# Written-out order of a fused Nyström attention and SiLU layer: transposes of batch 2 by DMA, scores in halves, loads and DMA transposes of a batch listed together

## The chip, the cores and the metric

The kernel runs on one core of a Trainium2 chip, as one launch. The metric is the time of the launch on the device in microseconds; the median of three runs is 250.57 us (249.38 to 251.9). A launch that was profiled beside them took 247.08 us; in it 245.4 us lie between the first and the last instruction of the program (the span), and 1.68 us outside. Times from the profile are counted from the start of the span.

## The reference

There are 8 batches (b = 0 to 7), 8 heads, 576 tokens, 64 numbers per head. q and k are averaged over groups of 18 tokens to 32 landmarks; three softmaxes A, Bm, C follow, six Newton steps towards an inverse of Bm, and a two-layer SiLU network on the result.

```python
q_lm = q.reshape(B, H, m, S // m, D).mean(axis=3)      # m = 32
k_lm = k.reshape(B, H, m, S // m, D).mean(axis=3)
A  = sm(q, k_lm)          # 576 x 32 per head
Bm = sm(q_lm, k_lm)       # 32 x 32
C  = sm(q_lm, k)          # 32 x 576
Z  = Bm.T / (...)
for _ in range(6):
    Z = 2 * Z - Z @ Bm @ Z
attn = A @ Z @ C @ v
# x: (4608, 512), all heads of a token side by side
h = x @ w_in              # 512 -> 2048
g = h * (1.0 / (1.0 + np.exp(-h)))
out = g @ w_out           # 2048 -> 512
```

## The kernel before

Heads go in two groups of four (g = 0, 1), so that 4 heads x 32 landmarks fill 128 partitions. Per batch the stages are:

- **Loads** (line 354, `load`): q and k (`ld0.b`, `ld1.b`, 576 KB each as bf16, line 400) and v in three parts (`ldv0.b` to `ldv2.b`, 192 KB each, line 407). They are issued by GpSimd (POOL), as are the first layer's weights (`wi...`, lines 414 and 418) and the second layer's (`wo0` to `wo3`, 512 KB each, line 424). Two buffers each for q/k, transposed q/k and v serve even and odd batches.
- **Transposes** of q and k into `qT`. For batches below `NTR` = 3 TensorE does them (`tr`, line 515: 18 for q and 18 for k, in four steps each) and ScalarE or VectorE copies them out of PSUM (`trc`). From batch 3 on, four DMA transposes per batch do them, issued by SyncE (SP): `xt10`, `xt11` for k and `xt00`, `xt01` for q (line 539). C's exponentials are transposed likewise: by TensorE in batches 0 and 1, by two DMA transposes `ct0`, `ct1` (line 814) after that.
- **Landmarks**: from batch 2 on a tree of four VectorE additions over the transposed k, then q (`lra` to `lrd`, line 575), then on TensorE `ltr1.b` and `ltr0.b` (one matmul `ps<-rs,fold` each).
- **Scores**: `sb` (Bm), `A` and `C` (16 matmuls `ps<-qT,lmT` each, four PSUM banks), exponentials `Ax`, `Cx`, column sums `S`, logarithms `Ln`, and the Newton steps `ns`, `nsd`, `fb`.
- **First layer with attention folded in**: `cv` (C times v), `zt`, `m` (into w_in), then 16 pieces `h` and two `hx` per batch, with SiLU by ScalarE (`g`, `gx`).
- **Second layer**: `o0` to `o3` for the first 256 rows of batch 0; all other rows as pairs of seven products `p1` to `p7` instead of eight, whose operand sums `ss` and `wt` VectorE makes.

What sets the order is `SEQUENCE` (line 19), written out by hand or by an earlier search: a list of the names above. `Plan.run` walks it, gives out PSUM banks, and emits each piece on its engine. So each engine's instructions stand in the list's order, and every engine works strictly in its own order; between engines only semaphores count, not places in the list. `*n` in the list is n matmuls on zeros, which keep TensorE busy at the start.

A few orderings between DMAs are added as waits (`after`). A DMA transpose of batch b waits until `ldv1.b` has landed; the loads of batch b+1 (line 1096, `later_loads`) wait for the third entry of batch b's list of DMA transposes, which is `xt00.b`, and from batch 4 on also for `ct0` of two batches earlier. No such wait ties the loads `wo0` to `wo3` to anything. In `load` there is also a dependence on the load eight before (lines 362 and 363); it is only asked about when the list is walked.

Of the kernel before, what the change touches and what calls it, by code (L numbers as in the profile page):

```python
# [10 lines left out]
AF = mybir.ActivationFunctionType  # L11
# [8 lines left out]
ldk ld11.0 const ident k0cACT k0cDVE k0 *15 lms100.0 tr15.0 tr10.0 trc10.0/DVE lms106.0 lms1012.0  # L20
*6 lms110.0 lms116.0 tr114.0 lms1112.0 lmc1.0/DVE ld00.0 *6 lms000.0 tr05.0 tr00.0 trc05.0/ACT
trc114.0/ACT ltr1.0 lmT1.0/ACT trc00.0/DVE tr19.0 trc19.0/DVE trc15.0/DVE lms006.0 ld01.0
lms0012.0 lms010.0 lms016.0 lms0112.0 ld0.1 ld1.1 ldv2.0 ldv0.0 wi0b1 ldv1.0 wi0b0 tr09.0 tr014.0
lmc0.0/DVE *1 ltr0.0 lmT0.0/ACT *6 sb.0 pb.0 trc014.0/DVE trc09.0/DVE A.0 Ax01.0 Ax00.0 Ax10.0
Ax11.0 *5 C.0 Cx01.0 Cx10.0 Cx11.0 Cx00.0 pbs.0 pbr.0 bmx.0 bmt.0 csb.0 n1.0 nrm.0 tr09.1 lms000.1
lms006.1 S10.0 lms0012.1 lms010.1 bbd.0 trc09.1/DVE stz.0 f0.0 stf0.0 stf1.0 fb00.0 lms016.1
Ln10.0 S00.0 Ln00.0 fb01.0 lms0112.1 lmc0.1/DVE S01.0 ns00.0 nsd00.0 Ln01.0 S11.0 ns01.0 Ln11.0
nsd01.0 fb11.0 ctm00.0 ctc00.0/DVE tr05.1 trc05.1/ACT tr00.1 trc00.1/ACT Rs1.0 Rs0.0 ns11.0
nsd11.0 fb10.0 fb21.0 tr19.1 trc19.1/DVE ltr0.1 lms100.1 lms106.1 ns10.0 nsd10.0 lms1012.1 tr014.1
lms110.1 lms116.1 trc014.1/DVE ns21.0 tr114.1 lmT0.1/ACT wi1a wi0a wi1b1 wi1b0 wi3b0 wi3a  # L30
lms1112.1 lmc1.1/ACT tr10.1 trc10.1/ACT tr15.1 *2 ltr1.1 lmT1.1/ACT fb20.0 nsd21.0 etn1.0
trc15.1/DVE ns20.0 fb31.0 *3 ns31.0 ctm10.0 trc114.1/ACT etn0.0 nsd31.0 sb.1 pb.1 *1 A.1 Ax01.1
Ax00.1 nsd20.0 fb30.0 pbs.1 wrc.0 *1 ns30.0 nsd30.0 ctc10.0/DVE fb40.0 pbr.1 fb41.0 bmx.1 bmt.1
wi3b1 Ax11.1 Ax10.1 *5 C.1 Cx00.1 Cx11.1 Cx01.1 *1 ns40.0 nsd40.0 ns41.0 nsd41.0 fb50.0 fb51.0
cv0.0 cv1.0 wc.0 S01.1 Ln01.1 ns50.0 nsd50.0 *2 ns51.0 bbd.1 nsd51.0 zbd.0 S11.1 Ln11.1 S00.1
Ln00.1 wi2b0 wi2b1 wi2a ldv0.1 ldv1.1 *5 zt.0 ztc.0/DVE S10.1 ctm00.1 ctc00.1/DVE Rs0.1 Ln10.1
Cx10.1 *2 m1.0 mc11.0/ACT mc10.0/DVE m0.0 f0.1 mc01.0/DVE mc00.0/ACT *1 ctm10.1 ctc10.1/DVE Rs1.1
csb.1 *1 h4.0 n1.1 m3.0 nrm.1 stz.1 stf0.1 mc31.0/DVE fb00.1 g4.0 mc30.0/DVE h2.0 g2.0 h6.0 g6.0
h0.0 g0.0 h3.0 ns00.1 wrc.1 nsd00.1 fb10.1 h5.0 g5.0 m2.0 mc21.0/ACT mc20.0/DVE *1 h13.0 g13.0
ns10.1 nsd10.1 fb20.1 h15.0 hx0.0 g15.0 ns20.1 nsd20.1 fb30.1 h9.0 g9.0 h11.0 g11.0 etn0.1 ns30.1  # L40
nsd30.1 fb40.1 hx8.0 gx8.0 g3.0 h8.0 h12.0 g12.0 etn1.1 ns40.1 nsd40.1 fb50.1 gx0.0 h10.0 g10.0
ld1.2 tr15.2 trc15.2/DVE h14.0 g14.0 ns50.1 nsd50.1 zbd.1 ldv2.1 cv0.1 wc.1 tr114.2 trc114.2/DVE
tr19.2 trc19.2/DVE zt.1 g8.0 ztc.1/ACT tr10.2 trc10.2/DVE lra1.2 h7.0 g7.0 m3.1 mc31.1/ACT
mc30.1/ACT m1.1 mc11.1/DVE mc10.1/ACT h1.0 g1.0 ld0.2 tr00.2 lrb1.2 tr09.2 tr014.2 trc014.2/DVE
tr05.2 trc05.2/DVE trc09.2/DVE lrc1.2 trc00.2/ACT h12.1 g12.1 h7.1 g7.1 h15.1 m2.1 mc20.1/ACT m0.1
mc00.1/ACT mc21.1/ACT mc01.1/ACT wo0 o0@5001.0 h14.1 g14.1 g15.1 o0@5000.0 fold lrd1.2 lra0.2
lrb0.2 lrc0.2 lrd0.2 h11.1 g11.1 ltr0.2 ltr1.2 lmT1.2/DVE lmT0.2/ACT ss00@5020.0 ss10@5020.0
ss20@5020.0 ss30@5020.0 wo1 h5.1 o1@5000.0 sb.2 pb.2 pbs.2 pbr.2 bmx.2 bmt.2 wo2 wt00 bbd.2 h8.1
h3.1 o1@5001.0 o2@5000.0 wo3 o2@5001.0 wt01 g8.1 csb.2 o3@5001.0 oc@5001.0/ACT g3.1 g5.1 n1.2
nrm.2 stz.2 o3@5000.0 hx8.1 f0.2 gx8.1 h0.1 g0.1 oc@5000.0/ACT h2.1 h10.1 g10.1 h4.1 h1.1 g2.1  # L50
g1.1 wt11 wt21 stf0.2 fb00.2 ns00.2 h13.1 g13.1 wt31 nsd00.2 fb10.2 wt10 wt20 wt30 p1@5020.0
c1@5020.0/ACT ns10.2 nsd10.2 fb20.2 h9.1 h6.1 g4.1 g9.1 g6.1 ss00@5100.0 p5@5020.0 c5@5020.0/DVE
hx0.1 gx0.1 ss10@5100.0 l1done.0 C.2 Cx00.2 Cx10.2 p6@5020.0 u2@5020.0/DVE ld1.3 ldv1.3 xt10.3
xt11.3 ns20.2 nsd20.2 ss20@5100.0 p3@5020.0 c12@5020.0 p7@5020.0 ld0.3 xt01.3 xt00.3 ldv0.2 ldv2.2
ldv1.2 l1done.1 A.2 Ax01.2 Cx11.2 ct1.2 Ax10.2 Ax11.2 p1@5100.0 c1@5100.0/ACT Ax00.2 Cx01.2 ct0.2
os@5000.0 ld1.4 lra1.3 fb30.2 ns30.2 p2@5020.0 ss30@5100.0 lrb1.3 os@5001.0 S10.2 S11.2 Ln11.2
Ln10.2 Rs1.2 p6@5100.0 S01.2 Ln01.2 S00.2 Ln00.2 p5@5100.0 nsd30.2 lrc1.3 fb40.2 lrd1.3 ltr1.3
c22@5020.0 lra0.3 u2@5100.0/DVE lrb0.3 p4@5020.0 ns40.2 lrc0.3 lrd0.3 ltr0.3 c11@5020.0 etn1.2
nsd40.2 c5@5100.0/ACT p3@5100.0 Rs0.2 lmT1.3/ACT etn0.2 lmT0.3/ACT sb.3 c12@5100.0 c21@5020.0/ACT
p7@5100.0 pb.3 pbs.3 pbr.3 fb50.2 A.3 Ax11.3 cv0.2 ldv1.4 c22@5100.0 wrc.2 wc.2 ld0.4 ldv0.3  # L60
ldv2.3 ldv2.4 ns50.2 nsd50.2 Ax10.3 Ax00.3 S11.3 Ln11.3 Ax01.3 p2@5100.0 C.3 Cx00.3 Cx01.3 Cx10.3
zbd.2 zt.2 ztc.2/ACT S10.3 Ln10.3 p4@5100.0 Cx11.3 ss00@5120.0 c11@5100.0 os@5100.0 ss10@5120.0
ss20@5120.0 p1@5120.0 S01.3 Ln01.3 m3.2 mc31.2/ACT bmx.3 wrc.3 mc30.2/DVE c21@5100.0/ACT os@5101.0
ct1.3 m2.2 mc21.2/DVE mc20.2/ACT bmt.3 p5@5120.0 S00.3 m0.2 m1.2 mc11.2/DVE csb.3 bbd.3 n1.3 nrm.3
stz.3 c1@5120.0/ACT p6@5120.0 u2@5120.0/DVE mc01.2/ACT mc10.2/ACT Rs1.3 Ln00.3 Rs0.3 mc00.2/ACT
h14.2 f0.3 h12.2 p2@5120.0 stf0.3 fb00.3 ns00.3 nsd00.3 c5@5120.0/DVE fb10.3 c11@5120.0 g12.2
p7@5120.0 h7.2 g7.2 ns10.3 nsd10.3 h4.2 h5.2 h8.2 g8.2 g5.2 fb20.3 ns20.3 h10.2 g10.2 c22@5120.0
p4@5120.0 c21@5120.0/ACT nsd20.3 fb30.3 ns30.3 hx0.2 nsd30.3 fb40.3 h15.2 gx0.2 g15.2 ns40.3
nsd40.3 ct0.3 xt00.4 ld1.5 ldv0.4 h9.2 g9.2 g14.2 h1.2 h0.2 g1.2 g0.2 cv0.3 ldv1.5 fb50.3
ss30@5120.0 ns50.3 wc.3 nsd50.3 zbd.3 ld0.5 h11.2 g11.2 h13.2 g4.2 g13.2 h3.2 g3.2 etn1.3 zt.3  # L70
ztc.3/DVE etn0.3 p3@5120.0 c12@5120.0 m3.3 mc30.3/ACT m0.3 mc01.3/DVE mc00.3/ACT m2.3 mc21.3/ACT
m1.3 mc20.3/ACT h2.2 hx8.2 g2.2 h6.2 g6.2 mc31.3/DVE h12.3 gx8.2 h3.3 h10.3 mc10.3/DVE mc11.3/DVE
h7.3 h2.3 g2.3 h4.3 g4.3 g10.3 h13.3 h5.3 g5.3 hx8.3 gx8.3 g13.3 h9.3 h11.3 g7.3 h14.3 h6.3 g6.3
g11.3 p1@5200.0 g3.3 h8.3 g8.3 ss00@5200.0 p5@5200.0 hx0.3 g14.3 g9.3 ss00@5220.0 xt11.4 xt01.4
xt10.4 ss10@5200.0 lra1.4 lrb1.4 lrc1.4 ss10@5220.0 ss20@5220.0 lrd1.4 lra0.4 lrb0.4 os@5020.0
ss20@5200.0 l1done.2 ltr1.4 h1.3 h0.3 g0.3 g1.3 g12.3 h15.3 gx0.3 c1@5200.0/DVE p6@5200.0
u2@5200.0/ACT os@5021.0 ss30@5200.0 c5@5200.0/DVE p3@5200.0 ss30@5220.0 lmT1.4/DVE lrc0.4 lrd0.4
ltr0.4 lmT0.4/ACT g15.3 p1@5220.0 sb.4 pb.4 c1@5220.0/ACT xt11.5 xt10.5 c12@5200.0 lra1.5 lrb1.5
lrc1.5 p7@5200.0 c22@5200.0 lrd1.5 p2@5200.0 c11@5200.0 p4@5200.0 c21@5200.0/ACT C.4 Cx11.4 Cx10.4
Cx01.4 p6@5220.0 u2@5220.0/ACT Cx00.4 p5@5220.0 c5@5220.0/ACT A.4 Ax01.4 Ax10.4 Ax00.4 Ax11.4  # L80
pbs.4 pbr.4 bmx.4 xt01.5 xt00.5 lra0.5 csb.4 ss00@5300.0 p1@5300.0 S10.4 ltr1.5 p7@5220.0 lrb0.5
ss10@5300.0 ss20@5300.0 lrc0.5 n1.4 nrm.4 wrc.4 lrd0.5 ltr0.5 lmT0.5/ACT S00.4 p3@5220.0 l1done.3
os@5120.0 os@5121.0 Ln10.4 os@5200.0 ct0.4 ld0.6 stz.4 c1@5300.0/ACT bmt.4 lmT1.5/DVE bbd.4 f0.4
sb.5 pb.5 stf0.4 S11.4 Ln11.4 Rs1.4 p2@5220.0 S01.4 Ln01.4 fb00.4 ns00.4 c22@5220.0 pbs.5
c11@5220.0 c12@5220.0 Ln00.4 p5@5300.0 c5@5300.0/ACT Rs0.4 p4@5220.0 c21@5220.0/ACT pbr.5
p6@5300.0 u2@5300.0/ACT etn1.4 ss30@5300.0 bmx.5 bmt.5 bbd.5 csb.5 etn0.4 nsd00.4 n1.5 fb10.4
ss00@5320.0 p3@5300.0 ss00@5340.0 ct1.4 cv0.4 ldv1.6 C.5 Cx00.5 Cx10.5 Cx11.5 Cx01.5 ns10.4
nsd10.4 p7@5300.0 p1@5320.0 nrm.5 fb20.4 ns20.4 wc.4 c12@5300.0 c22@5300.0 stz.5 nsd20.4 p2@5300.0
A.5 Ax10.5 Ax00.5 c1@5320.0/ACT p5@5320.0 ss10@5320.0 fb30.4 ns30.4 ss20@5320.0 f0.5 stf0.5
p4@5300.0 Ax01.5 Ax11.5 S11.5 Ln11.5 c21@5300.0/ACT p6@5320.0 u2@5320.0/ACT nsd30.4 fb40.4 ns40.4  # L90
S01.5 Ln01.5 ss30@5320.0 fb00.5 S10.5 p2@5320.0 Ln10.5 Rs1.5 nsd40.4 fb50.4 ns50.4 c11@5300.0
p7@5320.0 nsd50.4 zbd.4 zt.4 ss10@5340.0 ns00.5 nsd00.5 c11@5320.0 fb10.5 p1@5340.0 ztc.4/ACT
# [1070 lines left out]
```

## Time and profile before

| | us |
|---|---|
| median of three runs (lowest, highest) | 250.57 (249.38, 251.9) |
| the profiled launch | 247.08 |
| its span | 245.4 |
| ScalarE busy | 180.8 |
| VectorE busy | 180.0 |
| TensorE weight loads, beside matmuls | 165.8 |
| GpSimd busy | 36.7 |

Busy times are unions over an engine's instructions, so an engine that is busy 180 of 245 us may still be the bound in one stretch. A matmul's shown duration includes its way through the pipeline: what it costs in a dense row is the distance from its start to the next one's. The same holds for ScalarE and VectorE, whose neighbours overlap by about 0.1 us. Loads by GpSimd and stores and transposes by SyncE use the same 16 DMA engines through two queues, q0 and q1:

```profile
q0 software_dynamic: 15120, 18.06, 45.1%
q1 hardware_dynamic: 39808, 17.35, 34.9%
```

The columns are packets, megabytes, and the share of 16 engines' span.

### The profile page before, as it was taken

To read this page: it belongs to the slowest core of one execution; us is meant where nothing else is said; L and a number is where in the kernel's file an instruction comes from. 1 tells how busy PE (TensorE), PEld (TensorE's weight loads), DVE (VectorE), ACT (ScalarE), POOL (GpSimd) and SP (SyncE) were. 2 spreads that over 40 slices of the span, in tenths; PEclk is the share of its full clock that TensorE was granted. 3 is DMA by queue.
4 is the path that set the end of the run, shared out by engine and by line. 5 is a ranking of instruction groups with operands and counts; after the bars stand their busy time and mean duration, and the time that the engine had idled before them with its cause. 6 is when DMAs were issued, how large, how long until landed. Compare 5 with 4: busy or idle time off the path is not lost.

```text
span 245.4 us, 7471 instructions
## 1 busy us (share of the span) xinstructions
PE 233.3 (95%) x2948; PEld 165.8 (68%) x2948; DVE 180.0 (73%) x503; ACT 180.8 (74%) x432; POOL 36.7 (15%) x62
## 2 busy tenths in 40 slices
PE   7999999999999999199999999999999999999992
PEld 5986464457867556067878754777876765789882
DVE  2589889789998591489798968938899475348752
ACT  3299999988989998159746699999779788634100
POOL 8346713000050040000130060000000000000000
PEclk9999999999999999769999999999999999999999
DMA  6999999999999999793999999985414421012343
GB/s 160 207 203 197 206 207 206 210 205 204 132 177 220 202 137 178 185 194 98 136 190 171 167 185 239 190 145 136 108 47 117 121 52 39 1 43 77 88 119 109
DMA packets 55876, 36.84 MB, mean 150 GB/s; under 512 B 36640, under 2 KB 47392, under 8 KB 55840
## 3 DMA queue, kind: packets, MB, share of 16 engines
q0 software_dynamic: 15120, 18.06, 45.1%
q1 hardware_dynamic: 39808, 17.35, 34.9%
q10 hardware_dynamic: 912, 0.95, 1.4%
q8 instruction: 23, 0.38, 0.6%
q14 instruction: 13, 0.11, 0.1%
HBM read 36.70 MB, written 9.44 MB: 188 GB/s over the span
## 4 chain that ended last, share of the span: by engine, by line
PE 78%; ACT 7%; DMA 7%; SPq 3%; issue 1%; DVE 1%; ACTq 0%; DVEq 0%
PE ps L325 74%; DMA qT<-qk 6%; PE ps L515 3%; SPq L539 2%; ACT gm L913 2%; DMA gm<-in_k_dram 1%; ACT L913 1%; SPq L814 1%; ACT L1116 1%; ACT gx L936 1%; ACT m L335 1%; PE ps L802 1%; DVE red L575 1%; ACT pb L641 1%; ACT et L742 0%
## 5 line engine op out<-in xcount | busy, mean ns | idle before, releaser
L913 ACT ACTIVATE gm<-ps 128x512 f16<-128x512 f32 x128 | 68.7, 621 | 15.0 <-PE ps L325 14.3
L325 PE MATMUL ps<-etn,m 128*128 128x512 bf16 (+1 forms) x512 | 73.5, 289 | 0.2
L325 PEld LDWEIGHTS <-gm 128*128 128x128 f16 x512 | 48.6, 98 | 12.5 <-issue 1.3
L325 PE MATMUL ps<-w_out_sb,gm 128*128 128x256 f16 (+1 forms) x392 | 53.0, 281 | 0.0
L325 PEld LDWEIGHTS <-ss 128*128 128x128 f16 x408 | 39.5, 99 | 9.8 <-issue 1.8
L325 PEld LDWEIGHTS <-m 128*128 128x128 bf16 x512 | 31.5, 98 | 20.8 <-issue 3.2
L325 PE MATMUL ps<-wt,ss 128*128 128x256 f16 x272 | 35.5, 276 | 0.2
L1036 DVE TENSOR_TENSOR ost<-ost,ps 128x256 f32<-128x256 f32 x51 | 20.9, 416 | 13.4 <-PE ps L325 7.4
L335 ACT COPY ost<-ps 128x256 f32<-128x256 f32 (+1 forms) x45 | 17.2, 388 | 10.9 <-PE ps L325 10.6
L335 ACT CAST m<-ps 128x512 bf16<-128x512 f32 x36 | 19.4, 612 | 1.1 <-PE ps L325 0.8
L337 DVE CAST m<-ps 128x512 bf16<-128x512 f32 x28 | 18.3, 685 | 2.3 <-PE ps L325 1.9
L710 DVE SCALAR_TENSOR_TENSOR st<-st,ps 128x128 bf16<-128x128 bf16 (+2 forms) x54 | 13.6, 257 | 8.5 <-PE ps L325 5.5
L407 POOL DMA_DIRECT2D v<-in_v_dram x24 | 14.0, 590 | 30.8 <-DMA qT<-qk 13.6
L325 PE MATMUL ps<-w_out_sb,ss 128*128 128x256 f16 x136 | 17.5, 273 | 0.0
L325 PE MATMUL ps<-wt,gm 128*128 128x256 f16 x120 | 15.5, 272 | 0.0
L575 DVE TENSOR_TENSOR red<-qT 128x1024 f16<-128x1024 bf16 x12 | 8.3, 689 | 9.4 <-DMA qT<-qk 9.2
L685 DVE TENSOR_TENSOR fb<-st,hmask 128x256 bf16<-128x256 bf16 (+1 forms) x54 | 14.4, 271 | 0.8
L752 ACT ACTIVATE ln<-ps 128x288 f32<-128x288 f32 x32 | 12.4, 423 | 2.7 <-PE ps L325 2.4
L787 ACT ACTIVATE ce<-ps 128x288 bf16<-128x288 f32 x32 | 13.0, 424 | 1.7 <-PE ps L325 1.6
L1001 DVE TENSOR_TENSOR ss<-gm 128x1024 f16<-128x1024 f16 x15 | 10.2, 686 | 5.2 <-ACT gm L913 5.2
L742 ACT ACTIVATE et<-ps 128x288 bf16<-128x288 f32 x32 | 11.1, 423 | 3.6 <-PE ps L325 3.6
L337 DVE COPY ost<-ps 128x256 f32<-128x256 f32 x25 | 10.5, 420 | 3.2 <-PE ps L325 3.0
(93 smaller groups left out, 332.0 us busy)
## 6 DMA issues: line engine op xcount, KB each, us to landing
out_dram<-ost SPq DMA_DIRECT2D x126, 64.0 KB, 2.1
v<-in_v_dram POOLq DMA_DIRECT2D x24, 192.0 KB, 10.0
qk<-in_q_dram POOLq DMA_DIRECT2D x7, 576.0 KB, 10.6
qk<-in_k_dram POOLq DMA_DIRECT2D x7, 576.0 KB, 9.2
w_out_sb<-in_moe_w_out_dram POOLq DMA_DIRECT2D x4, 512.0 KB, 15.1
w_in_sb<-in_moe_w_in_dram POOLq DMA_DIRECT2D x8, 128.0 KB, 7.2
w_in_sb<-in_moe_w_in_dram POOLq DMA_DIRECT2D x4, 256.0 KB, 9.0
out_dram<-ost ACTq DMA_DIRECT2D x10, 64.0 KB, 1.7
```

The source lines that it names most:

```text
L325: nc.tensor.matmul(out=out_ap, lhsT=lhsT, rhs=rhs, start=start, stop=stop, skip_group_check=True)
L335: nc.scalar.copy(out=out, in_=in_)
L337: nc.vector.tensor_copy(out=out, in_=in_)
L407: lambda e, a=a: nc.gpsimd.dma_start(out=v_r[b % 2][a * L:(a + 1) * L, :, :], in_=v[b].rearrange("h (l a x) d -> a l h (x d)", l=L, a=VA)[ ...
L575: lambda e: nc.vector.tensor_tensor(out=o_, in0=a_, in1=b_, op=OP.add),
L685: nc.vector.tensor_tensor(out=fb[it % 2][:, g0:g1], in0=bc(sr[it % 3][:, g0:g1, 0:L], 4, 2), in1=bc(hmask, n, 1), op=OP.mult), [o], 14.5 + ...
L710: nc.vector.scalar_tensor_tensor(out=s2[:, g0:g1, lo:SW], in0=s[:, g0:g1, lo:SW], scalar=2.0, in1=ps[:, 0:NG * SW].rearrange("p (g x) -> p ...
L742: lambda e, g=g, et=et, c=c: nc.scalar.activation(out=et[:, c], in_=bank(me["A"], 2 * g + c)[:, 0:HS], func=AF.Exp, scale=sc / J),
L752: lambda e, g=g, c=c, ln=ln: nc.scalar.activation(out=ln[:, c], in_=bank(me["S", g, c])[:, 0:HS], func=AF.Ln),
L787: nc.scalar.activation(out=ce[:, :, 0:VP].rearrange("p (i c) (a l) -> p c a i l", c=2, a=VA)[:, c], in_=bank(me["C"], 2 * g + c)[:, 0:HS]. ...
L913: lambda e, dc=dc, cell=cell: nc.scalar.activation(out=gm[:, dc, :], in_=bank(cell["o"]), func=AF.Silu),
L1036: nc.vector.tensor_tensor(out=out_, in0=x, in1=y, op=OP.add)
```

## The change

`NTR` goes from 3 to 2, so batch 2 gets DMA transposes `xt10.2` to `xt01.2` in place of 36 TensorE transposes and 8 copies out of PSUM. `A` and `C` become two pieces per batch, one per head group, with two PSUM banks and 8 matmuls each. The dependence on the load eight before goes. Three estimates of duration, which only the list's maker uses, change. And the whole list is another one, with 56 matmuls on zeros instead of 64.

```diff
-    NTR = 3
+    NTR = 2
...
-        if len(swdge) >= 8:
-            d.append((swdge[-8], None))
...
-        use = [prev2[x] for x in ("A", "C") if x in prev2]
+        use = [prev2[x, g] for x in "AC" for g in range(NG) if (x, g) in prev2]
...
-        def am(e):
-            for g in range(NG):
+        for g in range(NG):
+            def am(e, g=g):
                 for h in range(4):
                     for c in range(2):
-                        mm(bank(me["A"], 2 * g + c)[L * h:L * h + L, 0:HS],
+                        mm(bank(me["A", g], c)[L * h:L * h + L, 0:HS],
...
-                    lmT_all + ([] if cr else [(pb_op, -0.2)]) + qt_ops[0, 0] + qt_ops[0, 1] + ready, p0 + 20,
-                    psum=4, tiled="q")
+                           lmT_all + ([] if cr else [(pb_op, -0.2)]) + qt_ops[0, g] + ready, p0 + 20,
+                           psum=2, tiled="q")
```

C changes in the same way. Of the list, the stretches around the two places that the prediction speaks of are these. Before, batch 2 and the second layer's weights:

```
... ld1.2 tr15.2 trc15.2/DVE h14.0 ... lra1.2 h7.0 ... ld0.2 tr00.2 lrb1.2 ...
... wo0 o0@5001.0 h14.1 g14.1 g15.1 o0@5000.0 fold lrd1.2 lra0.2
lrb0.2 lrc0.2 lrd0.2 h11.1 g11.1 ltr0.2 ltr1.2 lmT1.2/DVE ... wo1 ... wo2 ... wo3 ...
```

After:

```
... h7.1 g12.1 ld1.2 ld0.2 ldv0.2 ldv1.2 xt10.2 xt11.2 lra1.2 lrb1.2 lrc1.2 lrd1.2 xt00.2 xt01.2
lra0.2 lrb0.2 lrc0.2 lrd0.2 wo0 o0@5001.0 g9.1 h10.1 g10.1 h0.1 g11.1 g0.1 g2.1 g7.1 ss00@5100.0
ss10@5100.0 ss20@5100.0 ss30@5100.0 ltr1.2 lmT1.2/ACT wo2 wo1 wt00 o0@5000.0 o1@5000.0 o2@5000.0
ltr0.2 lmT0.2/ACT o1@5001.0 sb.2 pb.2 wo3 wt01 ...
```

SP's order of the transposes of batch 4 was `xt00.4 xt11.4 xt01.4 xt10.4`, with `ld1.5` listed right after the first; it becomes `xt10.4 xt11.4 xt00.4 xt01.4`, with `ld1.5 ld0.5 ldv0.5 ldv1.5 ldv2.5 ct0.4 ct1.4 cv0.4` in a row much later. GpSimd's order of loads becomes: k and q of batch 0, k and q of batch 1, `wi3` and v of batch 0, `wi2`, `wi0`, `wi1` and v of batch 1, then `ld1.2 ld0.2 ldv0.2 ldv1.2 wo0 wo2 wo1 wo3 ldv2.2 ld1.3 ...`.

## The prediction

> **What bounds the kernel now.** First the page's busy times and its 40 slices (6.1 us each; a digit is a tenth of the slice):
>
> ```profile
> PE 233.3 (95%) x2948; PEld 165.8 (68%) x2948; DVE 180.0 (73%) x503; ACT 180.8 (74%) x432; POOL 36.7 (15%) x62
> ...
> PE   7999999999999999199999999999999999999992
> ...
> PEclk9999999999999999769999999999999999999999
> ```
>
> TensorE (PE) is the bound throughout, with one hole in slice 17 and a lower granted clock in the two slices after. The waits of PE say what made the hole (total, times, longest):
>
> ```profile
> PE ps L325 <- DVE rs L575: 5.4, 1, 5.4
> ```
>
> The chain of waits (start, length, what) leads back from it:
>
> ```profile
> 86.72 14.41 DMA qT<-qk
> ...
> 101.23 0.70 DVE red L575
> ...
> 104.17 15.06 PE ps L325 x139
> ```
>
> A transpose of batch 4's k, `xt10.4`, was issued at 86.72 and took 14.41 us to land; the tree on VectorE (DVE) waited for it, `ltr1.4` for the tree. The table by stretches (length, then busy time and count of PE, PEld, DVE, ACT, POOL, granted clock, DMA share, GB/s) shows the price:
>
> ```profile
> 40.00:65.00 25.00, 25.00 (x235) 15.22 (x233) 21.73 (x58) 23.13 (x53) 1.16 (x2) 1.00 1.19 193
> 65.00:98.00 33.00, 32.79 (x444) 21.17 (x443) 23.24 (x64) 30.34 (x72) 6.31 (x10) 1.00 1.11 180
> 98.00:104.00 6.00, 0.75 (x19) 0.61 (x17) 2.70 (x6) 1.19 (x3) 0.00 (x0) 0.79 0.77 184
> 104.00:108.50 4.50, 4.33 (x16) 2.19 (x16) 4.40 (x11) 2.06 (x4) 0.00 (x0) 0.52 1.08 202
> ```
>
> Between starts of matmuls I count 5.6 us lost in the hole, and 2.0 us in the four pieces after it at half clock (three `h` at 0.85 instead of 0.43, one `p` at 1.58 instead of 0.87). The old stall is worth 7.6 us.
>
> Why did that transpose take so long? `ld1.5` waits for `xt00.4` alone, and that stood first on SP; so the loads of batch 5 (issued from 86.34) ran beside `xt10.4`, which stood last. Against it, how transposes go otherwise (issues by SP: start, length, count):
>
> ```profile
> 52.28 8.58 SPq L539 DMA_TRANSPOSE qT<-qk  x4
> ...
> 101.64 6.21 SPq L539 DMA_TRANSPOSE qT<-qk  x4
> ```
>
> The four from 101.64, with no load in flight, landed at 105.4, 106.9, 108.5 and 109.9. The four from 52.28 landed at 59.2, 60.2, 63.1, 64.1: three loads of v were still in flight until 58.2, and the first transpose came 1.0 us after them. `xt10.4` came 0.2 us after the last load beside it (100.9). In both rows a transposing DMA beside loads lands when the loads are through.
>
> **The change, part by part.**
>
> *The old stall.* In the new list `xt00` is third on SP, and `ct0` of two batches earlier is also waited for; only `xt01` can meet the next loads, and q's tree comes later than k's. I take the whole 7.6 us off.
>
> *36 transposes on PE.* 9 in 0.50 us, so 2.0 us; 8 matmuls on zeros fewer at 0.11 make 0.9. All of it lies before `ltr1.2`. The 8 copies (seven on DVE at 0.42 to 0.48, one on ACT at 0.59) also go, from a stretch where both are nearly full (21.73 and 23.13 of 25 us).
>
> *What takes their place* is the point of this prediction. `ltr1.2` now needs four DMAs and a tree, and the list cannot hold the weights' loads behind them: `wo0`, `wo2`, `wo1`, `wo3` have no wait on a transpose, and POOL issues them as early as the queue lets it. Here is how that went before, in POOL's timeline (start, length, count) and in the page's DMA issues (KB each, us to landing):
>
> ```profile
> 27.91 2.28 POOL L424 DMA_DIRECT2D w_out_sb<-in_moe_w_out_dram  x3
> 30.35 0.75 POOL L424 DMA_DIRECT2D w_out_sb<-in_moe_w_out_dram  x1 [0.16 <-issue]
> ```
>
> ```profile
> w_out_sb<-in_moe_w_out_dram POOLq DMA_DIRECT2D x4, 512.0 KB, 15.1
> ```
>
> They stand issued 12 to 18 us ahead of landing, in a queue that is full. So I add the queue up. Before, `ld0.2` landed at 37.8, then the four `wo` at 40.3, 42.9, 45.4, 47.9: 512 KB per 2.54 us, so 0.95 for a part of v. Now `ldv0.2` and `ldv1.2` come between: `ldv1.2` lands at 37.8 + 1.9 = 39.7, SP issues `xt10.2`, and behind `ldv1.2` 4 x 2.54 + 0.95 = 11.1 us of loads (the `wo` and `ldv2.2`) are already queued, to 50.8. That is the situation of 52.28 and 86.72, not that of 101.64.
>
> When does k's second transpose land? From below, as from 101.64: second landing 5.3 us after issue, at 45.0. By the row of 52.28: 1.0 us after the loads' end and another 1.0 for the second, 52.8. By the row of `xt10.4`, where 7.5 us of loads were stretched to 12.9: 11.1 x 1.72 = 19.1, loads end at 58.8, the second transpose at 60.8. Between 93 and 98 us the trace counts 719 packets of `xt10.4` and 673 of loads, about one for one. I take 54.3, nearer to the row of 52.28, which was also four at once. DVE then needs 1.7 us for the tree (0.70, 0.44, 0.29, 0.21 and hand-overs): `ltr1.2` at 56.0, from 46.7 to 62.5.
>
> The Trainium skill, "DMA: Bandwidth & Descriptors", section "Queues, rings and completion order", says that each DMA engine goes round between the queues that have work, a packet each; the one-for-one count agrees. If each of a transpose's 1,152 packets (counted in the trace) waits for one packet of `wo` on its engine, I estimate `ltr1.2` at 57.0 and the sum 1.0 us higher.
>
> PE would get there sooner. Before, `ltr1.2` started at 44.58. The new list puts eleven `h` (0.432 each) and an `hx` (0.466) of batch 1 ahead of it, 5.2 us, moves `o0@5000.0` (0.863) and `ltr0.2` (0.109) behind it and drops 2.9: PE arrives at 45.9, ACT's SiLU of those pieces perhaps 2 us later. So PE stands for 8 to 10 us. Behind `ltr1.2` on PE is everything else; behind `lra1.2` on DVE are q's tree, the operand sums `ss@5100` and `wt`. After such a hole the clock is at half for some 4 us: 2.0 us again.
>
> *The rest.* Half-size A and C are the same matmuls (16 in 0.37); ACT gets four more table loads (15 changes between exp and silu in the list instead of 11) of 1.28 us, all after `ltr1.2`, where ACT is busy 89% of the time or less; nothing, or 5.1 us if that cover is gone. The dropped dependence and the estimates emit nothing. One later place is tight: `ct0.3`, which can go 0.7 us after C's matmuls, gates the loads of batch 5 (3.9 us to land, some 10 for four loads), `ct0.4` and `ct1.4` wait for those (another 5), and `cv0.4` stands 20.2 us of PE work behind. That is 19.6 against 20.2: I take 1.0 us, from 0 to 4.
>
> **The sum.** Before, from the start of `ltr1.2` to the end of the last matmul (240.97) pass 196.4 us. Off go 7.6 of stall and, since more stands ahead of `ltr1.2`, 5.22 - 0.97 = 4.25. On come 2.0 of half clock and 1.0: 187.5. From 56.0 that ends at 243.5, 2.6 after 240.97. With the same end (6.1 us after the last matmul) the profiled launch would take 249.7 instead of 247.08, and the median 250.57 + 2.6 = 253.2.
>
> **The rivals.**
>
> 1. *Transposes are not held up* (decides if k's land by 44.2, so that PE never waits). For: the row from 101.64, and 1.4 us per issue. Against: both rows with loads in flight. Then `ltr1.2` is at 46.7 and without half clock: 253.2 - 9.3 - 2.0 = 241.9, faster by 3.5%. The Trainium skill says it this way, "Advanced Engine Details and Errata", section "X-Bar Transpose (TRN2)": on trn2 transposing DMAs are as fast as others. Beside loads, 14.41 us against 3.8 alone speak against it. Chance 0.2.
> 2. *Loads and transposes chase each other to the end*: every batch's `ct0` gates loads that gate the next `ct0` and `cv`. If the chain above takes 25 instead of 19.6, `cv0.4` and the stores behind it on SP (whose buffers `c1@5300` waits for) cost some 5 us with 2 of half clock: 260. For: 9.7 to 12.7 us for loads beside transposes at 86.34. Against: batches 6 and 7 have over 10 us of room. Chance 0.2.
> 3. *The change doesn't do what it says*: `xt01.4` and the next loads still overlap so that q's tree stalls PE in batch 4 as k's did; 253.2 + 7.6 = 260.8. Against: `ld1.5` also waits for `ct0.3`. Chance 0.05.
>
> **Numbers.** The forecast has 0.55. Its own range, from `ltr1.2` at 52 to 62.5, is 249 to 260. With the rivals the range is 244 to 261; rival 1 lies mostly below it, a little of rival 2 above. One per cent is 2.5 us, about what a measurement of this kernel can tell: slower by more than that means over 253.1, half of the forecast (0.29) and rivals 2 and 3 (0.25), together 0.54; within it 0.24 of the forecast and a little of rival 1; faster 0.21.
>
> **What would show it.** In the changed kernel's trace PE has one hole of 7 to 13 us that ends near 56 with `ps<-rs,fold`, released by DVE, itself by `DMA qT<-qk`; the time to landing of the first transposes is 10 us or more; half clock for about 4 us follows; the hole near 98 is gone. I am wrong in the main step if the first four transposes land within 6 us of their issue, wrong in the sum if other holes of over 2 us follow.

## The result and the profile after

| | before | after |
|---|---|---|
| median (lowest to highest), us | 249.97 (246.19 to 251.9) | 258.88 (258.29 to 260.2) |
| profiled launch, its span | 247.08, 245.4 | 258.29, 256.6 |

The median before is of four launches here, with one of 246.19 beside the three above. The kernel after takes 1.0455 times as long (interval 1.0322 to 1.0588). By the medians that is 8.9 us more, by the ratio some 11, where 2.6 were forecast. The 258.88 lie in the forecast's range; the size of the change was missed by more than a factor of three. Ratios here and below are formed without the launches that were slow (mostly those over 1.5% above the quickest of their kernel), the medians from all of them, so the two need not agree.

Busy times and slices (6.4 us each) of the kernel after:

```profile
PE 236.2 (92%) x2904; PEld 164.2 (64%) x2904; DVE 181.0 (71%) x498; ACT 185.1 (72%) x433; POOL 36.7 (14%) x62
...
PE   7799999819999999979993999999999999999993
...
PEclk9799999965999999999997799999999999999999
```

The old hole (slice 17 before) is gone, and there are two new ones: in slice 9, with half clock behind it, and in slice 22, with half clock again. TensorE's busy time is 2.9 above the one before, with 44 matmuls fewer; most of that is half clock, which cost 2.0 before and now 2.7, 2.1 and, for 3.4 us at the start, some 1.7. What TensorE waited for, and what its waits were put down to (total, times, longest):

```profile
PE ps L325 <- DVE rs L573: 6.5, 1, 6.5
PE ps L325 <- DVE ost L337: 4.4, 1, 4.4
PE ps L325 <- DMA qk<-in_k_dram: 2.6, 1, 2.6
PE ps L325 <- ACT ln L750: 1.3, 1, 1.3
```

The chain of waits (start, length, what) tells what stands behind the first, the last and the second of these:

```profile
43.59 11.50 DMA qT<-qk
...
55.18 0.70 DVE red L573
...
57.04 45.22 PE ps L325 x487
...
104.41 6.92 DMA out_dram<-ost
...
111.62 0.43 ACT ln L750
...
133.10 6.65 DMA out_dram<-ost
...
139.87 0.43 DVE ost L337
```

*The first hole* is the one forecast: k's second transpose of batch 2, then the tree, then `ltr1.2` at 57.04. *The other two links are stores.* VectorE or ScalarE copies a product out of PSUM into one of the output buffers; that copy waits until the buffer's last contents are stored; TensorE waits for the copy or for what stands behind it. SP's timeline shows why the stores were late (start of the first, length, count):

```profile
100.27 2.54 SPq L812 DMA_TRANSPOSE ct<-ce  x2
102.90 14.56 SPq L976 DMA_DIRECT2D out_dram<-ost  x8
117.58 2.54 SPq L812 DMA_TRANSPOSE ct<-ce  x2
120.21 4.31 SPq L537 DMA_TRANSPOSE qT<-qk  x3
124.63 3.07 SPq L976 DMA_DIRECT2D out_dram<-ost  x4
127.75 1.31 SPq L537 DMA_TRANSPOSE qT<-qk  x1
129.11 4.91 SPq L976 DMA_DIRECT2D out_dram<-ost  x9
```

The store `os@5120.0`, whose data were ready at 99.2, stands in SP's order behind `ct0.4`, `ct1.4` and the four transposes of batch 5. It was issued at 131.13, into the loads of batch 6 (`ld1.6` from 128.69), and landed at 139.75. `c1@5300.0` needs its buffer, TensorE the copy. Earlier `os@5021.0` was issued at 102.90, with the loads of batch 5 (from 103.41) right behind it, and landed at 111.33; `c5@5200` on ScalarE waits for that, and the logarithm that TensorE then waits for stands behind it.

The price by stretches (start and end, then length, busy time and count of PE, PEld, DVE, ACT, POOL, granted clock, DMA share, GB/s):

```profile
50.50:57.00 6.50, 0.08 (x1) 0.00 (x0) 1.70 (x4) 2.24 (x5) 0.38 (x1) 0.67 1.22 182
57.00:63.00 6.00, 5.96 (x16) 2.25 (x16) 5.36 (x10) 0.59 (x2) 2.75 (x5) 0.50 0.89 151
106.00:112.00 6.00, 4.56 (x109) 3.12 (x108) 3.69 (x15) 3.99 (x17) 1.73 (x3) 1.00 1.08 201
131.00:140.30 9.30, 4.94 (x28) 2.63 (x27) 4.44 (x9) 5.84 (x13) 0.82 (x2) 0.88 1.04 217
140.30:145.00 4.70, 4.65 (x22) 3.02 (x22) 2.65 (x5) 2.54 (x4) 0.00 (x0) 0.51 1.11 198
```

Between starts of matmuls, against the same pieces elsewhere: 6.6 in the first hole and 2.7 in the pieces at half clock after it; 1.6 at 110.5 to 112.3; 4.6 in the second hole and 2.1 at half clock after it. The start lost 2.7 as well: TensorE waited for k of batch 0 (`ld11.0`, landed at 8.29; 6.53 before). In this kernel that costs nothing, since `ltr1.2` waits for DMAs whenever TensorE arrives (*clean_dma* below shows it).

### The profile page after: what moved, and what is told of

Its sections match the earlier page's. It is cut to its first block, busy times and chain, and to the rows that moved or that the text cites. A ratio compares the mean times of both kernels' runs of the same rounds, so it can differ in the third digit from the quotient of the medians.

```text
span 256.6 us, 7397 instructions
## 1 busy us (share of the span) xinstructions
PE 236.2 (92%) x2904; PEld 164.2 (64%) x2904; DVE 181.0 (71%) x498; ACT 185.1 (72%) x433; POOL 36.7 (14%) x62
## 4 chain that ended last, share of the span: by engine, by line
PE 72%; DMA 12%; ACT 5%; DVE 4%; SPq 3%; issue 2%; DVEq 0%; ACTq 0%; POOLq 0%
PE ps L325 69%; DMA out_dram<-ost 5%; DMA qT<-qk 4%; ACT gm L911 3%; DMA qk<-in_k_dram 3%; SPq L976 3%; PE ps L513 2%; DVE m L337 1%; DVE red L573 1%; ACT m L335 1%; ACT gx L934 1%; DVE etn L759 1%; SPq L537 1%; DVE ost L337 1%; DVE st L708 0%
## 5 line engine op out<-in xcount | busy, mean ns | idle before, releaser
L911 ACT ACTIVATE gm<-ps 128x512 f16<-128x512 f32 x128 | 67.7, 660 | 5.7 <-PE ps L325 5.6
L325 PE MATMUL ps<-etn,m 128*128 128x64 bf16 (+1 forms) x512 | 71.0, 287 | 0.0
L325 PEld LDWEIGHTS <-gm 128*128 128x128 f16 x512 | 48.9, 99 | 21.0 <-issue 12.6
L325 PE MATMUL ps<-w_out_sb,gm 128*128 128x256 f16 (+1 forms) x392 | 56.3, 290 | 0.0
L325 PE MATMUL ps<-wt,ss 128*128 128x256 f16 x272 | 36.1, 281 | 4.4 <-DVE ost L337 4.4
L337 DVE CAST m<-ps 128x512 bf16<-128x512 f32 x31 | 20.3, 686 | 3.5 <-PE ps L325 3.1
L335 ACT CAST m<-ps 128x512 bf16<-128x512 f32 x33 | 18.1, 607 | 5.6 <-PE ps L325 5.5
L337 DVE COPY ost<-ps 128x256 f32<-128x256 f32 x27 | 11.3, 422 | 11.4 <-DMA out_dram<-ost 5.6
L398 POOL DMA_DIRECT2D qk<-in_k_dram x7 | 4.9, 707 | 100.6 <-DMA qT<-qk 37.1
L325 PE MATMUL ps<-wt,gm 128*128 128x256 f16 x120 | 15.6, 273 | 0.0
L785 ACT ACTIVATE ce<-ps 128x288 bf16<-128x288 f32 x32 | 13.6, 434 | 1.1 <-PE ps L325 1.1
```

Of the source, the lines that this page charges most:

```text
L325: nc.tensor.matmul(out=out_ap, lhsT=lhsT, rhs=rhs, start=start, stop=stop, skip_group_check=True)
L335: nc.scalar.copy(out=out, in_=in_)
L337: nc.vector.tensor_copy(out=out, in_=in_)
L785: nc.scalar.activation(out=ce[:, :, 0:VP].rearrange("p (i c) (a l) -> p c a i l", c=2, a=VA)[:, c], in_=bank(me["C", g], c)[:, 0:HS].rearr ...
L911: lambda e, dc=dc, cell=cell: nc.scalar.activation(out=gm[:, dc, :], in_=bank(cell["o"]), func=AF.Silu),
```

## The experiments

All times are medians in us; "before" is the kernel before, run beside it. Its own median moved from 248.4 to 251.6 between the three groups of runs, each on another chip; what moved it was not tried, so compare within a group first.

| | median (lowest to highest) | before | ratio (interval) |
|---|---|---|---|
| wo_gated | 261.58 (258.5 to 265.23) | 251.59 | 1.0347 (1.0201 to 1.0493) |
| tr_on_pe | 256.11 (254.38 to 258.17) | 251.59 | 1.0225 (1.0108 to 1.0342) |
| stores_early | 254.17 (252.83 to 255.36) | 251.59 | 1.0169 (1.0064 to 1.0274) |
| before_order | 244.49 (241.96 to 245.94) | 251.59 | 0.975 (0.9615 to 0.9884) |
| split_ac | 252.27 (248.07 to 253.41) | 248.41 | none formed |
| combo | 252.89 (250.2 to 256.23) | 248.41 | 1.013 (1.0043 to 1.0217) |
| fill | 255.87 (253.74 to 257.63) | 248.41 | 1.03 (1.0222 to 1.0378) |
| early_tr | 255.63 (254.65 to 256.75) | 248.41 | 1.032 (1.0255 to 1.0386) |
| clean_pe | 244.63 (243.63 to 247.96) | 250.51 | 0.9851 (0.9758 to 0.9944) |
| clean_dma | 252.79 (252.25 to 253.02) | 250.51 | 1.019 (1.0119 to 1.0262) |
| order_split | 244.75 (242.09 to 247.07) | 250.51 | 0.9835 (0.9744 to 0.9927) |
| before_order2 | 244.79 (243.82 to 245.53) | 250.51 | 0.9877 (0.9816 to 0.9938) |

### wo_gated: are the loads what makes the transposes slow?

```diff
+        if b == 2:
+            for x in wo_ops.values():
+                x.after = qt_ops[0, 1]
         if NPE <= b + 1 < B:
```

> The changed kernel, with the four loads of the second layer's weights held back until xt01.2 has landed. If transposes are slow because loads share the DMA engines: the four transposes of batch 2 land 5 to 9 us after the first is issued near 41.4, k's second by 47 instead of 55.1; the weights come late instead (54 to 62), so TensorE waits at o0@5001.0 and at o1 or o3 rather than at ltr1.2, and the time falls only to 254 to 258. If four transposes in a row from SyncE are slow in themselves: k's second still lands after 50, and the time rises above 262.

SP's timeline and the first wait of TensorE:

```profile
40.37 5.98 SPq L537 DMA_TRANSPOSE qT<-qk  x4
```

```profile
PE ps L325 <- DMA w_out_sb<-in_moe_w_out_dram: 5.8, 1, 5.8
```

The four transposes landed at 43.91, 45.58, 46.92 and 48.27: 7.9 us from the first issue, against 16.0 (41.39 to 57.35) beside the loads. So the loads are the cause. But `wo0`, now issued at 48.82, landed at 54.49, and `o0@5001.0` waited for it: the hole kept its size and changed its name. The time did not fall to the 254 to 258 that were expected; the two quickest launches took 258.5 and 258.7. The 2 MB of weights and the four transposes are wanted at the same time and use the same engines.

### tr_on_pe: batch 2 back on TensorE in the new list

`NTR = 3`; in the list `xt10.2 xt11.2` and `xt00.2 xt01.2` become the `tr`/`trc` of k and of q.

> The changed list with batch 2's transposes on TensorE again (36 matmuls, 8 copies), all else kept. If the hole of 6.5 us before ltr1.2 and the half clock after it (2.7) come from the DMA transposes alone: both go, 2.0 us of transposes come back, and the time is 258.9 - 9.2 + 2.0 = 251.7. If the new list is late there for another reason (the weights, or SiLU on ScalarE): a hole of 4 us or more stays between 45 and 60 and the time is 255 to 260.

```profile
PE ps L323 <- DVE ost L335: 3.8, 1, 3.8
PE ps L323 <- DMA qk<-in_k_dram: 2.3, 1, 2.3
PE ps L323 <- ACT ln L748: 2.2, 1, 2.2
PE ps L511 <- DVE qT L335: 1.8, 1, 1.8
```

The hole at `ltr1.2` is gone. The time is 4.4 over what was expected. Most of that is a new wait: in this list q's copies stand behind k's tree on VectorE (1.96, and some 1.7 of half clock). The stores' holes stay, as the expectation had it, at 2.2 and 3.8, each with half clock behind it, about a microsecond more than in the kernel after.

### stores_early: the stores out of the transposes' way

```diff
 # SP's order
-os@5020.0 os@5101.0 xt10.4 xt11.4 xt00.4 xt01.4 ct0.3 ct1.3 os@5021.0 os@5201.0
-ct0.4 ct1.4 xt10.5 xt11.5 xt00.5 os@5220.0 xt01.5 os@5121.0 os@5120.0 os@5200.0
+os@5020.0 os@5021.0 os@5101.0 xt10.4 xt11.4 xt00.4 xt01.4 ct0.3 ct1.3 os@5120.0 os@5121.0 os@5201.0
+ct0.4 ct1.4 xt10.5 xt11.5 xt00.5 os@5220.0 xt01.5 os@5200.0
```

> The changed kernel with three stores earlier on SyncE's queue: os@5021.0 right behind os@5020.0, os@5120.0 and os@5121.0 right behind ct1.3, ahead of the transposes that wait for the loads of batch 5. If the second hole (4.4 us at p6@5300.0, then half clock of 2.0) is the wait of c1@5300.0 for a buffer whose store stood behind those transposes: it goes, with some of the 2.4 us lost from 106 to 112, and the time is 250 to 253. If the stores only pass their delay on to ct0.4 and xt10.5: cv0.4 or ltr1.5 waits instead and the time is within 2 us of 258.9.

```profile
PE ps L322 <- DVE rs L570: 9.6, 2, 7.9
PE ps L322 <- DMA qk<-in_k_dram: 2.9, 1, 2.9
PE ps L322 <- DMA ct<-ce: 1.1, 2, 0.9
```

No wait for `ost` over a microsecond is left: `os@5120.0` was issued at 104.55 and landed at 112.67, well ahead of `c1@5300.0` at 135.95. The time fell by 4.7 from 258.88. The holes taken away were worth 8.2 (1.6 + 4.6 + 2.1); in this profiled run the first hole was larger (8.05 instead of 6.62), and later `ltr0.6` waited 1.8 and `cv0.6` 1.0 more.

### before_order: what the old stall was worth

```diff
 # SP's order of batch 4; ld1.5, ldv1.5, ld0.5 are listed behind it
-xt00.4 xt11.4 xt01.4 xt10.4
+xt10.4 xt11.4 xt00.4 xt01.4
```

> The kernel before with one thing of the change alone: batch 4's transposes in the order k, k, q, q, and the loads of batch 5 listed behind them. If the old hole is worth what the prediction took off (5.6 us and 2.0 of half clock): 242.4, no hole near 98, and xt11.4 lands within 6 us of xt10.4's issue. If the loads of batch 5, which now come later, are missed further on (cv0.5, ltr1.6): 246 to 251 with a new hole after 110.

```profile
PE   6999999999999989979999899997999999999992
...
PEclk9999999999999999999999999999999999999999
```

`xt10.4` landed 5.6 us after its issue instead of 14.4 (`xt11.4` landed 7.0 after that issue, where at most 6 were expected), the hole and the half clock are gone, and the kernel is 7.1 under the one before (5.7 when it was run again as *before_order2*). By the ratios it is 2.5 and 1.2%, some 6 and 3 us.

> before_order once more, beside order_split on the same chip: ratio to before 0.96 to 0.985 as the first time, 5 to 8 us under it.

So not all of the 7.6 comes out in the time. The profile of *before_order2* shows a wait of TensorE that was not there before, at 109.27. It is for an addition on VectorE that stands in the list behind the first steps of batch 5's tree, and those waited for their transpose:

```profile
PE ps L322 <- DVE ost L1033: 2.5, 1, 2.5
```

### split_ac and order_split: do scores in halves cost anything?

In the list before, each `A.b` becomes `A0.b A1.b` and each `C.b` becomes `C0.b C1.b`, with the code of the change for them; in *order_split* the same on *before_order*.

> The list of the kernel before with one thing of the change in it: A and C of every batch as two pieces of 8 matmuls and two banks, the two halves listed one behind the other where the whole stood; batch 2 is transposed on TensorE as before. My theory, as in the prediction: a half costs half, no engine gets more work, ratio to before 1.000, within 0.005. Rival: the pieces cost TensorE something of their own (a bank that is asked for later, a switch between pieces): 16 pieces more at 0.1 to 0.2 us make 1.6 to 3.2 us, ratio 1.006 to 1.013. The other rival: banks go back in twos instead of fours, and the kernel gains, ratio under 0.995.

> before_order (the list before with batch 4's transposes in the order k, k, q, q ahead of the loads of batch 5), with A and C in halves as in split_ac. split_ac was 3.9 slower than before, and its trace put that on the old hole (9.70 instead of 5.58) and its half clock. If that was the old hole's own scatter, it is gone here and the halves cost nothing: same time as before_order2 within 0.5%, ratio to before 0.97 to 0.98. If the halves cost something of their own: 3 to 4 us over before_order2.

The median of *split_ac* was 3.9 over the kernel before, where equality within 0.5% was expected. Its quickest launch (248.07) lies among those of the kernel before (245.86 to 248.91 for nine of twelve). The trace, of a launch of 253.05, has a larger old hole:

```profile
PE ps L323 <- DVE rs L571: 9.5, 1, 9.5
```

That hole was 5.4 in the kernel before: here the loads of batch 5 ended at 105.36 instead of 100.90, and `xt10.4` with them. Where the old hole is taken away, halves and wholes are equal: 244.75 and 244.79. So the halves cost nothing there. Why five of six runs of *split_ac* (252.1 to 253.4), but only three of the twelve of the kernel before (251.96 to 253.5), lay that high, was not tried further. That the hole's own scatter spreads the kernel before from 245.86 to 253.52 is likely, not shown: without the hole *before_order2* spreads only from 243.82 to 245.53, but *order_split* from 242.09 to 247.07.

### early_tr: transposes issued 5 us earlier

On *stores_early*, batch 2's transposes no longer wait for `ldv1.2`, only for the k or q that they read:

```diff
-            gate = v_ops[b][-2:-1]
+            gate = v_ops[b][-2:-1] if b > 2 else []
```

> stores_early with the transposes of batch 2 not waiting for ldv1.2; they still wait for the k or q that they read. Theory of sharing by packets: a transpose takes long because the loads in flight get every second packet, and starting 5 us earlier (36 to 37 instead of 41.4 to 43) it also ends some 5 us earlier: first landing 48 to 50, second by 51, ltr1.2 at 52 to 54, the hole 1.5 to 4 instead of 8.05, and 4 to 7 us off the time: 247 to 250. Rival, that a transpose beside loads lands when the loads are through, whenever it was issued: landings at 54 to 58 as before, since the loads are not sooner through with more beside them; ltr1.2 at 57 to 59, time 254, same as stores_early.

```profile
36.41 20.75 SPq L534 DMA_TRANSPOSE qT<-qk  x4
```

The first was issued at 36.41 and landed at 49.58, after 13.2 us, as sharing packet by packet would have it. The second, issued at 38.66 and until 49.58 behind the first on the same queue, landed at 57.17; the last load beside it, `ldv2.2`, landed at 57.16. `ltr1.2` came at 59.12. The rival is right where it counts: the second transpose lands when the loads are through. The time, 255.63, is no better than the 254.17 of *stores_early*: the earlier issue gained nothing while the same bytes were wanted at the same time.

### fill: work put into the hole

```diff
-... ss30@5100.0 ltr1.2 lmT1.2/ACT wo2 wo1 wt00 o0@5000.0 o1@5000.0 o2@5000.0 ltr0.2 lmT0.2/ACT o1@5001.0 sb.2
+... ss30@5100.0 wo2 wo1 o0@5000.0 o1@5000.0 o2@5000.0 o1@5001.0 ltr1.2 lmT1.2/ACT wt00 ltr0.2 lmT0.2/ACT sb.2
```

> stores_early with four pieces of batch 0's second layer (o0, o1, o2 of the first 128 rows, o1 of the second; 0.863 each) listed ahead of ltr1.2 instead of behind it; the transposes by DMA stay and are as late. My theory: the hole is the distance between what TensorE has to do and the landing of k's second transpose; ltr1.2 starts where it did in stores_early (58 to 59), the hole shrinks by 3.45 from 8.05 to about 4.6, half clock stays about 2: 254.17 - 3.45 = 250.7, ratio 1.0 of before. Rival: the weights wo2 and wo1 come too late as well (they share the engines with the transposes), so that the pieces wait for them and the hole only changes its name: 253 to 254, with DMA w_out_sb<-in_moe_w_out_dram as releaser.

Neither came. The hole at `ltr1.2` shrank, as I had said (4.71 lost, `ltr1.2` at 58.31), but `ltr0.2` then waited 2.2 for q's tree and the piece behind it 0.75 for ScalarE's copy: 7.65 together, against 8.05. Where they stood before, behind `ltr1.2`, the four pieces had given q's tree that time (there `ltr0.2` did not wait). And a hole of 3.9 appeared at `ltr0.5`, with half clock behind it:

```profile
PE ps L322 <- DVE rs L570: 10.3, 3, 4.5
```

### combo: both causes out at once, and what was left

The stores as in *stores_early*, and batch 2 on TensorE with k's copies and tree, then q's, ahead of the four `ss@5020` on VectorE; the transposes are spread out among the `h` of batches 0 and 1.

> The kernel after, its list otherwise kept, with both causes taken out together: batch 2's q and k transposed by TensorE (copies by VectorE, the trees of k and q right behind them and the four operand sums ss@5020 behind the trees, so that nothing but copies stands ahead of a copy), and the three stores early as in stores_early. My theory, that the two causes are separate and make up the whole loss: from the 254.17 of stores_early go the first hole (8.05) and its half clock (1.9), 2.0 come for the transposes: 246.2, ratio 0.98 of before, with no wait of TensorE over 2.7 us (the one at the start is left). Rival: the new list is slower for other reasons too, and taking both out leaves it at or above the kernel before: 250 or more, ratio 0.995 or more, with new waits of TensorE on copies near 45 to 52.

252.89 instead of 246.2: a third cause showed itself, the one that *fill* also had (there the fourth transpose came 0.45 ahead of the load and took 6.5). SP's timeline:

```profile
118.31 4.17 SPq L535 DMA_TRANSPOSE qT<-qk  x3
122.61 2.20 SPq L974 DMA_DIRECT2D out_dram<-ost  x4
124.88 1.31 SPq L535 DMA_TRANSPOSE qT<-qk  x1
```

The load `ld1.6` waits for the third transpose of batch 5 alone and was issued at 125.12, 0.24 after the fourth, which a store had held up. That fourth transpose took 6.43 us (landed 131.31), q's tree came late and `ltr0.5` cost 3.8 and some 1.4 at half clock. In *stores_early* the fourth stood 1.3 ahead of the load and took 3.2. This is the prediction's rival 3, one batch later than it was looked for. The start (3.0 and half clock) now counts as well, since no wait for DMAs behind it absorbs it, `tr09.2` waited 1.8 for a copy, and `cv0.4` 1.5 for `ct0.4`.

### clean_pe and clean_dma: the change's own idea in a clean list

Both have these edits more; *clean_pe* is *combo* with them, *clean_dma* is *stores_early* with them.

```diff
 # SP's order
-xt10.5 xt11.5 xt00.5 os@5220.0 xt01.5
+xt10.5 xt11.5 xt00.5 xt01.5 os@5220.0
 # the start
-const ... ld00.0 ident ... lms1012.0 lms110.0 lms116.0 lms1112.0 tr10.0 tr15.0
+const ident ... ld00.0 ... lms1012.0 tr10.0 tr15.0 *8 lms110.0 lms116.0 lms1112.0
```

> combo with two more edits. (1) SP's store os@5220.0, which stood between the third and the fourth transpose of batch 5, goes behind the fourth (xt01.5). (2) The start: two transposes of batch 0 and eight matmuls on zeros go ahead of lms110.0, and the identity is built ahead of the load ld00.0, as in the list before. My theory: in combo xt01.5 came 0.2 us before the load ld1.6 and took 6.43 us instead of 3.2, that made the second hole (3.80 and 1.4 of half clock); and the start lost 3.04 and 1.7 of half clock at lms110.0, of which the eight matmuls cost 0.9 again. 252.89 - 5.2 - 3.8 = 243.9, ratio 0.975 to 0.985 of before, xt01.5 landing in 3 to 4 us, no wait of TensorE over 2 us. Rival: behind xt01.5 the next thing is just as late (the stores, ct0.4), ltr0.5 or p6@5300.0 waits again and the time stays at 250 or more.

> The same two edits on stores_early, with batch 2's q and k still transposed by DMA: against clean_pe this has only the change's own idea, 36 transposes and 8 copies in exchange for four DMAs. If the hole at ltr1.2 is the price of that idea: ltr1.2 at 57 to 59 whatever was gained at the start, hole 8 to 9, half clock about 2, no second hole: 251 to 254, that is 7 to 10 over clean_pe. Rival: with a better list the transposes come in time and save their 2 us: 242 to 246, not over clean_pe.

Busy times and slices of *clean_pe*, then the first waits of *clean_dma*:

```profile
PE 232.3 (96%) x2948; PEld 163.5 (67%) x2948; DVE 184.0 (76%) x506; ACT 185.6 (77%) x433; POOL 36.7 (15%) x62
...
PE   7899999799999999999999999999999999999992
...
PEclk9999999999999999999999999999999999999997
```

```profile
PE ps L322 <- DVE rs L570: 9.8, 2, 9.3
PE ps L322 <- DVE zer L429: 1.1, 1, 1.1
```

Both expectations hold in the main. In *clean_pe* no slice has a hole, `xt01.5` landed in 3.28 us, and the longest wait is 1.6, for a copy of batch 2. In *clean_dma* TensorE is done with its other work sooner than in the kernel after (`h0.1` at 48.24 instead of 49.99), and `ltr1.2` still starts at 58.15: the gain ahead of it goes into the wait. The hole is 9.5 (8 to 9 were expected) and half clock behind it costs 2.9. The one exchange between the two, with the places in the list that go with it, costs 8.2 us.

So the new list is not worse in itself: 258.88 less 4.7 (stores), 1.4 (the fourth transpose and the start) and 8.2 (batch 2 by DMA) is *clean_pe*, as fast as *before_order*. Both are quicker than the kernel after and, by 1.2 to 2.5% with intervals that stay below 1, than the kernel before. Listing the weights' loads ahead of those of batch 2, so that no load runs beside the transposes, was not tried.

## Why the prediction was right and where it failed

**The old stall, 7.6.** Right for this list: it is gone after, and the stretch from `ltr1.2` to the last matmul closes with it (196.4 - 7.6 - 4.25 + 2.7 + 8.2 = 195.5; measured 195.6). It is not a price that holds in any list: taken out of the old one, 7.1 and 5.7 came out by the medians, some 6 and 3 by the ratios, where that other wait came in its place.

**The new hole, `ltr1.2` at 56.0.** Right in place, releaser and cause: 57.04. That the moment came out within 1.0 is partly luck. `ldv1.2` landed at 41.23 instead of 39.7, since `ld0.2` ahead of it landed at 39.43 and not at 37.8 as in the list before; from there to k's second landing (55.09) it took 13.9 us, where the forecast had 14.6. The loads ended at 54.06, 12.8 us after `ldv1.2` (11.1 by the queue alone, 19.1 by the row of `xt10.4`); the first transpose landed with them (54.02) and the second 1.0 after, where the row of 52.28 has the first 1.0 and the second 2.0 after. (In that row `ld0.3` was in flight too, to 55.07, beside the three loads of v.) The hole was 6.6 instead of 8 to 10, because TensorE stood from 50.5 on instead of 45.9 to 48: the start had lost 2.7, and ScalarE is on the chain from 32 to 43.

The Trainium skill ("DMA: Bandwidth & Descriptors", section "Queues, rings and completion order") has each engine alternate between queues by packets. The trace agrees: between 47 and 50 us it counts 478 packets of the transposes' queue and 476 of the loads'. The estimate of 57.0 met 57.04 by the same luck, as it had 15.6 us where 13.9 were measured, and the second landing of *early_tr*, expected by 51 from such sharing, came at 57.17. The Trainium skill ("Advanced Engine Details and Errata", section "X-Bar Transpose (TRN2)") has transposes as fast as other DMAs; that agrees with *wo_gated* (four in 7.9 us) and not with a transpose beside loads (12.6 us for one).

**What that exchange costs.** Forecast and rival 1 differ by 9.3 of hole and 2.0 of half clock; less the 2.0 of transposes on TensorE that is 9.3. *clean_dma* against *clean_pe* gives 8.2, and *clean_pe* still pays 1.8 for a late copy.

**Half clock, 2.0 after the hole.** 2.7.

**Halves of A and C, 0.** Right, by *order_split*.

**The later tight place, 1.0 (0 to 4).** This is the step that failed. I followed one chain, `ct0.3`, the loads of batch 5, `ct0.4`, `cv0.4`, and priced it at 1.0 because it closed in 19.6 of 20.2 us. `cv0.4` did not wait: it started at 123.16, 1.75 after `ct1.4` had landed (in *combo*, with less to hold TensorE up ahead of it, it waited 1.5). So the chain that was priced was sized about right. What the sum had at nothing were the stores that the new list puts behind those transposes on SP, and the copies that need their buffers: 1.6 before 112, then 4.6 and 2.1 of half clock at 135.7, 8.2 in the profile for the 1.0 in the sum, and 4.7 in time when *stores_early* takes them away. Rival 2 had named the buffer (`c1@5300`) and the price (5 and 2 of half clock), but as an alternative to the forecast, with a late `cv0.4` as its condition. It needed none: a store whose data are ready at 99 and which stands behind six transposes is late by the list alone, and it came on top of the forecast. The order of SP's stores was in the list before the run, and the prediction moved only the loads and transposes past each other.

**The sum.** Last matmul at 252.66 instead of 243.5: 1.0 from `ltr1.2`, 0.7 of half clock, 8.2 - 1.0 from the stores; together 8.9 of the 9.2. From profile to profile the loss is 11.2, as by the ratio. The medians show 8.9; the profiled launch before (247.08) was at the quick end of a kernel whose launches scatter.

**What would show it.** One hole ending near 56, first landing 10 us or more, the old hole gone: all there, though the hole, at 6.6, lies just under the 7 to 13 and half clock lasted 5.9 us instead of 4. "Wrong in the sum if other holes of over 2 us follow": there was one.

## What to carry to other kernels

On a queue that works in order, list every instruction that is moved past another, the stores too, and ask of each when its data are ready and who waits for its buffer; a store behind transposes behind loads is late by all three. A transposing DMA lands soon where no load is in flight beside it (3.5 us here, 12.6 beside loads); issuing it earlier, or holding the loads back, only moved the wait, since the same bytes were due at the same time. Behind a wait for DMAs the gain ahead of it is lost, and a cause that is covered by a larger one shows only when that one is gone: measure causes together as well as one by one.

## What was not expected of the hardware

- *Stores suffer like transposes.* Four 64 KB pieces of a store landed 3.0 us after the first issue with no loads beside them (`os@5401.0`), and 8.4 and 8.6 us with them (`os@5021.0`, `os@5120.0`).
- *A transpose in the middle of loads can be held to their end.* 18.5 us from issue to landing in *early_tr*, 10.9 of them behind the first transpose, where four alone took 7.9.
- *Issue distances of less than a microsecond decide.* `xt01.5` 1.3 us ahead of the next load (*stores_early*) or 0.8 ahead (*early_tr*): 3.2 us; 0.45 ahead (*fill*): 6.5; 0.24 ahead (*combo*): 6.4.
